# Layer 0's second MLP pair: the right sums' quarters spread over six points, two of them in the pair ahead

## The chip, the cores and the metric

One NeuronCore of a Trainium2 chip runs the whole program. The metric is the device time of one execution in microseconds, taken as the median of several runs; less is better. A profile of one execution is read beside it, and its times count from the first instruction of that execution.

## The reference, cut to what matters

Two layers of each block are run in turn on a tensor x of 2048 x 512: a Fourier mixing block (A) and a token-shift block with an MLP (B).

```
A(x):  a, b = x @ dft_hid_re.T, x @ dft_hid_im.T          # 512 x 512
       y    = dft_seq_re @ a - dft_seq_im @ b              # 2048 x 2048
B(x):  h  = gelu(LN(x) @ w1);  hs = shift(h) @ w2;  x1 = x + hs
       h2 = gelu(LN(x1) @ w3) @ w4;                        # 512 x 1376, 1376 x 512
       return x1 + h2
x = x + A(LN(x));  x = x + B(LN(x));  x = x + A(LN(x));  x = x + B(LN(x))
```

The change touches the end of B in layer 0, where the MLP runs, and there a side job that prepares matrices for A of layer 1.

## The kernel before, in words

**Number format.** Every matrix product is made of three TensorE matmuls (`mm3`, L343 to L345): an operand is split into a high part (a rounding copy on ScalarE, "highs", a CAST in the trace) and a low part (the difference, a subtraction on VectorE, "lows").

**The MLP in pairs.** The 2048 tokens are four chunks of 512, worked in two pairs. In a pair the hidden products of w3 are formed by a seven-product scheme: a period (one turn of `for p in range(NF // 2)`, five in a pair) makes the products b1, b6, b5, b2, b7, then one or two parts of the product with w4 (`w4_part`, T1 and T2 below; the first period has one), then b4 and b3. Each product is six matmuls in the trace into one of four PSUM banks, which are used in turn. A bank comes free when its reader has run: b1 is copied by ScalarE (`u`, L1329), the others are added by VectorE (L567, tile `rest`): `v = u + b6`, `x = v + b5`, `u = u + b2`, `v = v + b7`, `y = v + b5`, later `v = v + b4`, `x = x + b3`. Since four banks go round, b7 waits for the copy of b1, b4 for `v = u + b6`, b3 for `y = v + b5`; the next period's b1, b6, b5 and b2 wait for the additions of b2, b7, b4 and b3.

**The points.** Each engine runs its instructions in the order in which the code is written. Side work is put into that order at points: `one()` takes the next entry of the list `bg`. The second pair has 26 points, 0 to 25: 0 and 1 ahead of the first period, then in each period A (behind the issue of b5), B (behind b7 and its two additions), C and D (behind T1 and T2; the first period has no D) and E (behind b3). So A to E are 2, 3, 4, -, 5 in period 0; 6 to 10 in period 1; 11 to 15, 16 to 20, 21 to 25 in periods 2, 3 and 4. The entries of `bg` there are `lows("t4")` and the list `early`, which normalizes the first rows of the next layer (`xp_stats`, L357 to L363; `xp_norm`, L391; `ax_sums`, L422; `ax_lows`, L448; `ay_sums`, L427).

**The right sums.** `hs_forms` and `hs_quarter` make, in four quarters, seven matrices (`hsd`, in DRAM) out of the four blocks of the hidden DFT matrix; layer 1 reads them from 800 us on. A quarter loads two tiles `m` (blocks b11, b12) and `r` (b21, b22) of 256 KB each (L1210, L1213), forms four sums (L567, output `hp..f` or `hs`), and puts out seven results: high (L1226), low (L1231), and a store of 256 KB to `hsd` (L1232). The results pass through three small buffers `fp[0]`, `fp[1]`, `fp[2]` which lie at the same three places for all quarters; a buffer may be written again only when its store has landed. All transfers are issued by SP, in order, among them the loads of w4 (`w4_load`, L945, 512 KB) and of w3 (`w3_load`, L960, 1792 KB, one at the end of each of the first three periods, ahead of the work of point E).

**Before, a quarter takes five points**, quarter n at points 5n to 5n + 4: the four sums at the first; three highs, the point's own entry and three lows at the second; two results at the third, one each at the fourth and fifth. The loads of the next quarter stand at the end of the fourth (`m`) and fifth (`r`) point. Quarter 0's loads stand in the first pair, in `then[9]`. The list `then` holds work for the first pair's last parts: `then[k + 2]` runs behind part k.

Of the kernel before, what the change touches and what calls it, by code (L numbers as in the profile page):

```python
# [11 lines left out]
ALU = mybir.AluOpType  # L12
# [7 lines left out]
CH = 512  # L20
# [3 lines left out]
DH = D // 2  # L24
# [21 lines left out]
def spectral_mlp_kernel(ctx: ExitStack, tc: tile.TileContext, x, ws, hs, w1, w2, w34, out):  # L46
# [18 lines left out]
    hsd = [[dram.tile([P, 2, CH], F32, name=f"hsd{i}{j}") for j in range(2)] for i in range(7)]  # L65
# [17 lines left out]
    RAWS = EXT + 6 * D  # L83
    STG = RAWS + RAW * 2 * CH + 32
# [3 lines left out]
    def at(name, word, *shape, dtype=F32R):  # L88
        return nc.alloc_sbuf_tensor_at(name, [P, *shape], dtype, offset=base + 4 * word).ap()

    def both(name, word, *shape):
        return at(name, word, *shape), at(name + "f", word, *shape, dtype=F32)
# [134 lines left out]
    raws, slots, sums, place = {}, {}, {}, {}  # L227
# [9 lines left out]
    def rows(sb, d, j, n, load):  # L237
        v = d[j * P : (j + n) * P, :].rearrange("(t p) d -> p t d", p=P)
        nc.sync.dma_start(*((sb, v) if load else (v, sb)))
# [287 lines left out]
    def low(tf):  # L527
        nc.vector.tensor_tensor(tf[0][:, :, 1], tf[1][:, :, 1], tf[0][:, :, 0].bitcast(F32), op=ALU.subtract)
# [37 lines left out]
    def add(o, a, b, op=ALU.add):  # L566
        nc.vector.tensor_tensor(o, a, b, op=op)  # L567
# [292 lines left out]
    def by_pairs(layer, zs, xin, dst):  # L860
# [51 lines left out]
        def sum_of(*names):  # L912
            return lambda: b_sum(*names)
# [4 lines left out]
        def highs(*names):  # L918
            return lambda: [high((blk[b], blkf[b])) for b in names]

        def lows(*names):
            return lambda: [low((blk[b], blkf[b])) for b in names]
# [32 lines left out]
        def w3_load(n):  # L955
            if n >= n_pairs * (NF // 2):
                return
            if layer or n >= NF // 2:
                i = (n + (last_of(layer) and n >= NF // 2)) % 2
                nc.sync.dma_start(w3b[i].bitcast(F32), w3d[n % (NF // 2)])  # L960
                return
            nc.sync.dma_start(staged.rearrange("p f k w -> p f (k w)"), w34[2 * n : 2 * n + 2, :, 0].rearrange("f p w -> p f w"))
# [116 lines left out]
        steps = [(shifted, 0, g) for g in GORDER]  # L1079
# [32 lines left out]
        bg, prep = [], {}  # L1112
# [9 lines left out]
        def do_all(*fs_):  # L1122
            return lambda: [f() for f in fs_]
# [22 lines left out]
        def next_steps():  # L1146

            steps = (
                ((ay_lows, 2), (ay_sums, 3), (ay_highs, 3), (more, 1)),
                ((ay_lows, 3),),  # L1150
                ((xp_stats, 4), (keep_rows, 8)),
                ((xp_stats, 5), (more, 2)),
                ((xp_norm, 4),),
                ((xp_sums, 4), (xp_highs, 4), (more, 3)),
                ((ax_lows, 4), (xp_norm, 5)),
                ((ay_lows, 4), (ax_sums, 5), (ax_highs, 5), (more, 4)),
                ((ax_lows, 5), (keep_rows, 10)),
                ((ahead, 1), (more, len(pieces))),
                ((ahead, 1),),
                ((ahead, 1),),  # L1160
                (),
            )
            return [[do(*s)] for s in steps]
# [30 lines left out]
            ]  # L1194

        def hs_forms():
            steps = []
            for n in range(4):
                d, v = n // 2, slice(n % 2, n % 2 + 1)
                m, r = (at(f"hs{i}{n}", RAWS + (1 + i) * CH, 1, CH, dtype=F32) for i in range(2))  # L1200
                fp = [both(f"hp{i}{n}", word, 1, 2, DH) for i, word in enumerate((RAWS + 3 * CH, STG, STG + CH))]
                steps += hs_quarter(m, r, fp, [(t[d][:, v], hs[(1, d)][:, v], hs[(0, d)][:, v]) for t in hsd])
            return steps

        def hs_quarter(m, r, fp, places):
            b11, b12, b21, b22 = (t[:, :, v] for t in (m, r) for v in (left, right))
            raw = [tf[:, :, 1] for _, tf in fp]

            def load_m():
                nc.sync.dma_start(m, places[0][1])  # L1210

            def load_r():
                nc.sync.dma_start(r, places[0][2])  # L1213

            def sums():
                add(raw[1], b12, b11, ALU.subtract)
                add(raw[2], b22, b12, ALU.subtract)
                add(raw[0], b22, raw[1], ALU.subtract)
                add(b12, raw[0], b21, ALU.subtract)

            def outs(*which):
                which = [(i, n, raw[i] if src is None else src) for i, n, src in which]

                def highs_():
                    for i, _, src in which:
                        act(fp[i][0][:, :, 0], src)  # L1226

                def lows_():
                    for i, n, src in which:
                        t = fp[i][0]  # L1230
                        nc.vector.tensor_tensor(t[:, :, 1], src, t[:, :, 0].bitcast(F32), op=ALU.subtract)  # L1231
                        nc.sync.dma_start(places[n][0].rearrange("p i (l w) -> p i l w", l=2), t.bitcast(F32))  # L1232

                return highs_, lows_

            nothing = lambda: None
            parts = [
                (nothing, sums),
                outs((1, 3, None), (2, 4, None), (0, 2, None)),
                outs((1, 0, b11), (2, 1, b12)),  # L1240
                outs((0, 6, b21)),
                outs((1, 5, b22)),
            ]
            return [(load_m, load_r), *parts]

        def next_block(c, half, to):
            return lambda: b_in(c, half, to)
# [12 lines left out]
        for pair in range(n_pairs):  # L1260
# [10 lines left out]
            if next_too:  # L1271
                hcs[8:] = [hx[:, 0], hx[:, 1], rest[0]]
                bg += [lows("t4"), *early]
                for n in range(4):
                    parts = work[6 * n + 1 : 6 * n + 6]
                    for i, (before, behind) in enumerate(parts):
                        more_ = []
                        if n < 3 and i > 2:
                            more_.append(work[6 * n + 6][i - 3])
                        bg[5 * n + i] = do_all(before, bg[5 * n + i], behind, *more_)  # L1280
            elif pair:
                bg.append(lows("t4"))
            sets = [rest[4:8], rest[4:8]]
# [6 lines left out]
            for i, names in enumerate((("11", "21"), ("12", "22"))):  # L1290
                for d in range(KD):
                    b = blk[names[d // 2]]
                    v = slice(d * P, (d + 1) * P)
# [12 lines left out]
            def next_blocks(*which):  # L1306

                for c, half, to in which:
                    b_in(c, half, to)
# [13 lines left out]
            for p in range(NF // 2):  # L1323
                prep = {} if kept else w_prep(p)
                u, v, x, y = sets[p % 2]
# [49 lines left out]
            then = [[] for _ in range(NF + 2)]  # L1375
            if pair == 0:
                work = hs_forms()
                then[9] = [*work[0]]
                next_blocks((3, 1, "22"))
                then[1] = [lambda: w3_load(NF // 2)]  # L1380
                then[2] = [lambda: rows(xs[0], dst, 0, 2, False)]
                then[3] = [lambda: rows(xs[1], dst, 2, 2, False)]
                then[4] = [sum_of("t1", "12", "11"), sum_of("t2", "22", "t1")]
                then[5] = [sum_of("t3", "22", "12"), sum_of("t4", "21", "t2"), highs("11", "21")]
                names = "11", "21", "12", "22", "t2", "t1", "t3", "t4"
                for i in range(6):
                    then[6 + i] += [lows(names[i]), highs(names[i + 2])]
                then[8] += [lambda: w3_load(NF // 2 + 1)]
                then[12] = [lows("t3")]
            if next_too:  # L1390
                then = next_steps()
            if next_too:
# [497 lines left out]
    for layer in range(LAYERS):  # L1890
# [4 lines left out]
        for c in range(NC):  # L1895
            if layer == 0 and c == 0:
# [22 lines left out]
                def second_low(i):  # L1919
# [5 lines left out]
                parts = [  # L1925
                    [(halves[0][:, 1], mid[0][:, 0], 1), (halves[0][:, 0], ay[0][:, 2], 0)],
                    [(halves[1][:, 0], mid[0][:, 1], 0), (halves[1][:, 1], ay[0][:, 3], 1)],
                ]
# [156 lines left out]
        for i, (ri, dp) in enumerate(HORDER):  # L2085
# [17 lines left out]
            if i == 2:  # L2103
                run_late("re0")
                low(z_half(0, 1))
        by_pairs(layer, zs, xin, out if last_layer else x2d)


# [53 lines left out]
```

## Time and profile before

| what | us |
|---|---|
| median of 3 runs (1448.34 to 1449.6) | 1449.16 |
| the profiled execution, device time | 1448.9 |
| its span, first to last instruction | 1446.9 |
| TensorE matmul busy | 1422.4 (98%) |
| VectorE busy | 1203.9 (83%) |
| ScalarE busy | 731.8 (51%) |

The difference between device time and span, 2.0 us, lies around the program. The second MLP pair of layer 0 runs its periods from 614.7 to 687 us of the span.

In the rows of the profile PE is TensorE, DVE VectorE, ACT ScalarE, POOL GpSimd, and SPq the queue of transfers that SP issues. A row of the timeline gives start, duration, engine, line, operation, output<-inputs, shapes and, in brackets, the idle time before it with what ended it. `hp12f` is the first buffer-written sum of quarter 2, `rest` the tiles u, v, x, y, `psa` and `psd` the four PSUM banks of the products.

### The profile page before, as it was taken

To read this page: it belongs to the slowest core of one execution; us is meant where nothing else is said; L and a number is where in the kernel's file an instruction comes from. 1 tells how busy PE (TensorE), PEld (TensorE's weight loads), DVE (VectorE), ACT (ScalarE), POOL (GpSimd) and SP (SyncE) were. 2 spreads that over 40 slices of the span, in tenths; PEclk is the share of its full clock that TensorE was granted. 3 is DMA by queue.
4 is the path that set the end of the run, shared out by engine and by line. 5 is a ranking of instruction groups with operands and counts; after the bars stand their busy time and mean duration, and the time that the engine had idled before them with its cause. 6 is when DMAs were issued, how large, how long until landed. Compare 5 with 4: busy or idle time off the path is not lost.

```text
span 1446.9 us, 18506 instructions
## 1 busy us (share of the span) xinstructions
PE 1422.4 (98%) x6681; PEld 1190.4 (82%) x6681; DVE 1203.9 (83%) x1725; ACT 731.8 (51%) x1020; POOL 76.7 (5%) x105
## 2 busy tenths in 40 slices
PE   9999999999999999998999999999989999999998
PEld 7888888888888888876888888888877888899887
DVE  7986998989978887677889879879879797897676
ACT  6663454455566654354555434444345656444342
POOL 2100000000002000000000001000000021000000
PEclk9999999999999999999999999999999999999999
DMA  7867657568645858867656667577686447576864
GB/s 253 271 206 237 199 172 262 173 198 297 228 133 155 280 202 286 340 222 282 232 166 211 203 233 248 189 258 250 219 288 234 161 116 262 172 249 219 318 202 165
DMA packets 145628, 325.24 MB, mean 225 GB/s; under 512 B 10624, under 2 KB 61568, under 8 KB 142848
## 3 DMA queue, kind: packets, MB, share of 16 engines
q1 hardware_dynamic: 145536, 324.05, 66.9%
q8 instruction: 53, 0.87, 0.2%
q14 instruction: 39, 0.32, 0.1%
HBM read 262.41 MB, written 61.60 MB: 224 GB/s over the span
## 4 chain that ended last, share of the span: by engine, by line
PE 79%; DVE 10%; DMA 4%; ACT 3%; issue 2%; SPq 0%; POOL 0%; DVEq 0%; ACTq 0%; POOLq 0%
PE psd L343 8%; PE psd L345 8%; PE psd L344 8%; PE psa L344 7%; PE psa L343 7%; PE psa L345 6%; PE psb L344 6%; PE psb L345 6%; PE psb L343 6%; PE psc L344 6%; PE psc L345 6%; PE psc L343 6%; DVE ring L300 2%; DMA raw<-in_ws 1%; DVE rest L567 1%
## 5 line engine op out<-in xcount | busy, mean ns | idle before, releaser
L300 DVE TENSOR_TENSOR ring<-raw,ring 128x1024 fp32r<-128x1024 f32 x102 | 124.2, 1220 | 19.1 <-ACT ring L279 19.0
L279 ACT CAST ring<-raw 128x1024 fp32r<-128x1024 f32 x103 | 107.9, 1051 | 55.0 <-PE psd L345 24.9
L383 POOL TENSOR_TENSOR rs<-ve,mhalf 128x4 f32<-128x4 f32 x16 | 26.9, 1684 | 741.0 <-DVE nm L382 741.0
L300 DVE TENSOR_TENSOR ring<-ring1f,ring 128x512 fp32r<-128x512 f32 (+1 forms) x56 | 53.3, 952 | 2.9 <-ACT ring L282 2.9
L286 ACT CAST ring<-ring2f 128x1024 fp32r<-128x1024 f32 x28 | 29.6, 1056 | 49.9 <-DVE ring2f L285 49.9
L343 PE MATMUL psd<-rawr,hf 128*128 128x256 f32 x168 | 49.1, 292 | 5.8 <-issue 4.8
L286 ACT CAST ring<-ring0f 128x1024 fp32r<-128x1024 f32 x28 | 29.5, 1053 | 47.0 <-DVE ring0f L285 46.6
L391 ACT ACTIVATE tmp<-xs,nb,rs 128x512 f32<-128x512 f32 x56 | 43.3, 809 | 19.0 <-POOL nb L363 13.5
L343 PE MATMUL psc<-ring,ay 128*128 128x512 f32 x128 | 50.0, 391 | 2.2 <-ACT rr11f L610 2.2
L362 POOL TENSOR_TENSOR rs<-ve,mhalf 128x2 f32<-128x2 f32 (+2 forms) x33 | 29.6, 898 | 425.4 <-DVE nb L361 406.5
L344 PE MATMUL psb<-ring,ay 128*128 128x512 f32 x128 | 49.9, 390 | 2.2 <-DVE ring L300 2.2
L300 DVE TENSOR_TENSOR ring<-ring3f,ring 128x1024 fp32r<-128x1024 f32 (+1 forms) x50 | 49.3, 986 | 3.1 <-ACT ring L282 2.6
L344 PE MATMUL psc<-ring,ay 128*128 128x512 f32 x128 | 49.9, 390 | 0.6 <-DVE ring L300 0.6
L343 PE MATMUL psd<-ring,ay 128*128 128x512 f32 x126 | 49.4, 392 | 0.6 <-DVE tmp L567 0.6
L345 PE MATMUL psc<-ring,ay 128*128 128x512 f32 x128 | 49.8, 389 | 0.0
L343 PE MATMUL psb<-ring,ay 128*128 128x512 f32 x128 | 49.8, 389 | 0.0
L345 PE MATMUL psb<-ring,ay 128*128 128x512 f32 x128 | 49.8, 389 | 0.0
L344 PE MATMUL psd<-ring,ay 128*128 128x512 f32 x126 | 49.0, 389 | 0.0
L344 PE MATMUL psa<-ring,ay 128*128 128x512 f32 x126 | 49.0, 389 | 0.0
L345 PE MATMUL psd<-ring,ay 128*128 128x512 f32 x126 | 49.0, 389 | 0.0
L343 PE MATMUL psa<-ring,ay 128*128 128x512 f32 x126 | 49.0, 389 | 0.0
L345 PE MATMUL psa<-ring,ay 128*128 128x512 f32 x126 | 49.0, 389 | 0.0
(896 smaller groups left out, 4763.6 us busy)
## 6 DMA issues: line engine op xcount, KB each, us to landing
raw<-in_ws SPq DMA_DIRECT2D x183, 512.0 KB, 5.3
w4r<-w4d SPq DMA_DIRECT2D x44, 512.0 KB, 5.2
rawr<-hsd SPq DMA_DIRECT2D x42, 512.0 KB, 4.8
w3b<-w3d SPq DMA_DIRECT2D x10, 1792.0 KB, 9.5
raw<-in_hs SPq DMA_DIRECT2D x32, 512.0 KB, 3.9
w3d<-w3b SPq DMA_DIRECT2D x5, 1792.0 KB, 7.0
hsd<-hp SPq DMA_DIRECT2D x28, 256.0 KB, 2.5
x1d<-tmp SPq DMA_DIRECT2D x12, 512.0 KB, 7.4
```

What stands on the lines that cost most here:

```text
L279: nc.scalar.copy(dest[:, a:b, 0], r[0][:, a:b])
L286: nc.scalar.copy(dest[:, :, 0], lo)
L300: nc.vector.tensor_tensor(lo, src, hi.bitcast(F32), op=ALU.subtract)
L343: nc.tensor.matmul(o, lh, rh, start=first, stop=False, skip_group_check=more)
L344: nc.tensor.matmul(o, lh, rl, start=False, stop=False, skip_group_check=more)
L345: nc.tensor.matmul(o, ll, rh, start=False, stop=last, skip_group_check=more)
L362: nc.gpsimd.tensor_tensor(rs[:, :n], ve[:, :n], mhalf[:, 0, :n], op=ALU.pow)
L383: nc.gpsimd.tensor_tensor(rs, ve, mhalf[:, :, :2], op=ALU.pow)
L391: nc.scalar.activation(o, s, AF.Identity, bias=mr[2], scale=mr[1])
L567: nc.vector.tensor_tensor(o, a, b, op=op)
```

## The change

A quarter is cut into six parts. The first sum (b12 - b11, into `fp[0]`) stands alone; the next part puts that result out, with the other three sums between its high and its low; the remaining parts put out two, one, two and one results. Quarter n begins at point 6n - 2, so that quarter 0 has its first two parts in the first pair (`then[11]` and `then[12]`), and the others start at points 4, 10 and 16. The three buffers change roles from quarter to quarter (`words[(i + n) % 3]`). The next quarter's `m` is loaded ahead of the point before its first part, and `r` behind that point's work. The numbers of instructions are unchanged on every engine.

```
         def hs_forms():
-            steps = []
+            work = []
...
-                fp = [both(f"hp{i}{n}", word, 1, 2, DH) for i, word in enumerate((RAWS + 3 * CH, STG, STG + CH))]
-                steps += hs_quarter(m, r, fp, [(t[d][:, v], hs[(1, d)][:, v], hs[(0, d)][:, v]) for t in hsd])
-            return steps
+                words = (RAWS + 3 * CH, STG, STG + CH)
+                fp = [both(f"hp{i}{n}", words[(i + n) % 3], 1, 2, DH) for i in range(3)]
+                work.append(hs_quarter(m, r, fp, [(t[d][:, v], hs[(1, d)][:, v], hs[(0, d)][:, v]) for t in hsd]))
+            return work
...
+            def first_sum():
+                add(raw[0], b12, b11, ALU.subtract)
+
             def sums():
-                add(raw[1], b12, b11, ALU.subtract)
-                add(raw[2], b22, b12, ALU.subtract)
-                add(raw[0], b22, raw[1], ALU.subtract)
-                add(b12, raw[0], b21, ALU.subtract)
+                add(raw[1], b22, b12, ALU.subtract)
+                add(raw[2], b22, raw[0], ALU.subtract)
+                add(b12, raw[2], b21, ALU.subtract)
...
             parts = [
-                (nothing, sums),
-                outs((1, 3, None), (2, 4, None), (0, 2, None)),
-                outs((1, 0, b11), (2, 1, b12)),
-                outs((0, 6, b21)),
-                outs((1, 5, b22)),
+                ((), (first_sum,)),
+                ((high_,), (sums, low_)),
+                part((1, 4, None), (2, 2, None)),
+                part((0, 0, b11)),
+                part((1, 1, b12), (2, 6, b21)),
+                part((0, 5, b22)),
             ]
...
-                for n in range(4):
-                    parts = work[6 * n + 1 : 6 * n + 6]
+                ahead_, behind_ = [[] for _ in bg], [[] for _ in bg]
+                for n, (load_m, load_r, parts) in enumerate(work):
+                    at_ = 6 * n - 2
+                    if n:
+                        ahead_[at_ - 1].append(load_m)
+                        behind_[at_ - 1].append(load_r)
                     for i, (before, behind) in enumerate(parts):
-                        more_ = []
-                        if n < 3 and i > 2:
-                            more_.append(work[6 * n + 6][i - 3])
-                        bg[5 * n + i] = do_all(before, bg[5 * n + i], behind, *more_)
+                        if at_ + i >= 0:
+                            ahead_[at_ + i] += before
+                            behind_[at_ + i] += behind
+                bg[:] = [do_all(*f, g, *h) for f, g, h in zip(ahead_, bg, behind_)]
...
-                then[9] = [*work[0]]
+                then[9] = [*work[0][:2]]
...
-                then[12] = [lows("t3")]
+                then[11] += work[0][2][0][1]
+                then[12] = [*work[0][2][1][0], lows("t3"), *work[0][2][1][1]]
```

How the order of instructions moves at three places. First VectorE at the end of the first pair, ahead of the additions of its last result into the rows (`xs`, L1110); `hs_4384` is quarter 0's m, `hs_4385` its r, and `bt_..` are operands of the second pair.

```order
 L528 TENSOR_TENSOR bt_228<-bt1f,bt_228 128x2x512
+L567 TENSOR_TENSOR hp00f<-hs_4384 128x256
 L528 TENSOR_TENSOR bt_232<-bt3f,bt_232 128x2x512
+L567 TENSOR_TENSOR hp10f<-hs_4385,hs_4384 128x256
+L567 TENSOR_TENSOR hp20f<-hs_4385,hp00f 128x256
+L567 TENSOR_TENSOR hs_4384<-hp20f,hs_4385 128x256
+L1234 TENSOR_TENSOR hp_4386<-hp00f,hp_4386 128x256
 L1110 TENSOR_TENSOR xs_165<-psc_285,xs_165 128x512
```

Four sums and one low now stand ahead of the additions into the rows; before, none of them did.

Second VectorE in period 3 (points A, B and C of the last quarter's start); `xs_166` is the row tile that `xp_stats` reads, `rest_..` the additions x, u, v, y, and `hp03f`, `hp13f`, `hp23f`, `hs_4408` the sums of quarter 3. The first rows are the end of its statistics.

```order
 L361 TENSOR_SCALAR nb<-mv 128x2
-L1231 TENSOR_TENSOR hp_4412<-hp13f,hp_4412 128x256
-L1231 TENSOR_TENSOR hp_4414<-hp23f,hp_4414 128x256
-L1231 TENSOR_TENSOR hp_4410<-hp03f,hp_4410 128x256
+L567 TENSOR_TENSOR hp03f<-hs_4408 128x256
 L567 TENSOR_TENSOR rest_278<-rest_277,psd_287 128x512
 L567 TENSOR_TENSOR rest_276<-rest_276,psa_280 128x512
 L567 TENSOR_TENSOR rest_277<-rest_277,psa_281 128x512
 L567 TENSOR_TENSOR rest_279<-rest_277,psd_287 128x512
```

Three lows leave this place; the first sum of quarter 3, which reads that quarter's m, now stands ahead of the four additions x, u, v and y.

Third SP at the end of period 2, around the last load of w3 (`w3b_238<-w3d_87`); `hs_4408` and `hs_4409` are m and r of quarter 3.

```order
 L945 DMA w4r_249<-w4d_117 128x1024
-L1232 DMA hsd_100<-hp_4404 128x512
-L1213 DMA hs_4409<-in_hs 128x512
+L1235 DMA hsd_92<-hp_4404 128x512
+L1235 DMA hsd_102<-hp_4406 128x512
 L960 DMA w3b_238<-w3d_87 128x3584
-L1232 DMA hsd_96<-hp_4412 128x512
-L1232 DMA hsd_98<-hp_4414 128x512
-L1232 DMA hsd_94<-hp_4410 128x512
+L1211 DMA hs_4408<-in_hs 128x512
+L1235 DMA hsd_100<-hp_4402 128x512
+L1214 DMA hs_4409<-in_hs 128x512
```

Before, both loads of quarter 3 were issued ahead of the load of w3; now both stand behind it. Those of quarters 1 and 2 stand ahead of their period's load of w3 in both kernels.

More of the change, by code (lines that the diff above doesn't have):

```diff
@@ L1234, in outs, with part @@
                 return highs_, lows_
-            nothing = lambda: None
+            def part(*which):
+                high_, low_ = outs(*which)
+                return (high_,), (low_,)
+            high_, low_ = outs((0, 3, None))
             parts = [
-                (nothing, sums),
-                outs((1, 3, None), (2, 4, None), (0, 2, None)),
-                outs((1, 0, b11), (2, 1, b12)),
-                outs((0, 6, b21)),
-                outs((1, 5, b22)),
+                ((), (first_sum,)),
[4 more added lines that the diff above has]
+                part((0, 5, b22)),
             ]
-            return [(load_m, load_r), *parts]
+            return load_m, load_r, parts
         def next_block(c, half, to):
```

## The prediction

> **What bounds the kernel now.** I read first the page's shares, then the stretch of the second pair in windows, then who waited for whom there. TensorE is busy 98% of the span, so only its idle time and its slow time can be won.
>
> ```profile
> PE   1422.4 (98%) x6681; PEld 1190.4 (82%) x6681; DVE 1203.9 (83%) x1725; ACT 731.8 (51%) x1020; POOL 76.7 (5%) x105
> ```
>
> (The page's own first line; the next two are windows, with busy time and instruction count of each engine, then clock.)
>
> ```profile
> 600.00:638.00 38.00, 38.00 (x169) 31.48 (x168) 25.82 (x51) 14.01 (x26) 1.09 (x3) 1.00 0.66 243
> 615.00:690.00 75.00, 69.18 (x288) 55.42 (x287) 55.36 (x122) 36.90 (x73) 4.02 (x8) 0.95 0.71 249
> ```
>
> The first window has no stall: 169 matmuls in 38.00 us, 0.225 us each. The second holds the five periods: its 288 matmuls would need 64.8 of the 75 us, so about 10 us are lost. Where, the timeline of TensorE shows (start, duration, the idle time in brackets):
>
> ```profile
> 641.41 0.50 PE L343 MATMUL psa<-b,w3b 128*128 128x512 f32 x1 [0.74 <-DVE rest L567]
> 646.43 0.50 PE L343 MATMUL psa<-bt,w3b 128*128 128x512 f32 x1 [0.64 <-DVE rest L567]
> 660.68 0.80 PE L343 MATMUL psa<-b,w3b 128*128 128x512 f32 x1 [3.07 <-DVE rest L567]
> 661.27 0.63 PE L344 MATMUL psa<-b,w3b 128*128 128x512 f32 x1
> ...
> 666.39 0.56 PE L344 MATMUL psd<-bt,w3b 128*128 128x512 f32 x1
> 666.79 0.39 PE L345 MATMUL psd<-bt,w3b 128*128 128x512 f32 x1
> 679.47 0.50 PE L343 MATMUL psd<-b,w3b 128*128 128x512 f32 x1 [0.73 <-DVE rest L567]
> 684.50 0.50 PE L343 MATMUL psd<-bt,w3b 128*128 128x512 f32 x1 [0.64 <-DVE rest L567]
> ```
>
> Five times PE waits for an addition `rest` that frees a bank. The first, third and fourth are b3 waiting for `y`, the others the next b5 waiting for `v + b4`. The idle time sums to 5.8 us; the third stall is dearer than it looks, because behind 3.07 us of idleness the 14 matmuls from 660.68 to 666.79 stand 6.1 us apart instead of 3.2. With about 0.3 us more at the refilling behind each short stall (0.50 us for its first matmul), the loss is 5.8 + 2.9 + 1.3 = 10.0 us, as the count says.
>
> Why are the additions late? The waits of this stretch (engine, line, waited for: total, times, longest):
>
> ```profile
> DVE hp12f L567 <- DMA hsd<-hp: 3.7, 1, 3.7
> DVE hp13f L567 <- DMA hsd<-hp: 3.2, 1, 3.2
> DVE hp11f L567 <- DMA hsd<-hp: 2.4, 1, 2.4
> ACT hp L1226 <- DMA hsd<-hp: 4.9, 5, 3.2
> DVE hp23f L567 <- DMA hs<-in_hs: 0.2, 1, 0.2
> ```
>
> Once a quarter VectorE stands at the first sum until the store that last used its buffer has landed, and everything behind it in order, the additions too, is late by as much. For quarter 2:
>
> ```profile
> 652.99 0.43 DVE L567 TENSOR_TENSOR hp12f<-hs 128x256 f32<-128x256 f32 x1 [3.71 <-DMA hsd<-hp]
> 653.53 0.43 DVE L567 TENSOR_TENSOR hp22f<-hs,hs 128x256 f32<-128x256 f32 x1
> 655.27 1.28 DVE L357 BATCH_NORM_STATS2 st<-xs 128x6 f32<-128x512 f32 x2
> 657.02 0.42 DVE L1231 TENSOR_TENSOR hp<-hp12f,hp 128x256 fp32r<-128x256 f32 x1
> 659.94 0.69 DVE L567 TENSOR_TENSOR rest<-rest,psa 128x512 f32<-128x512 f32 x1
> ```
>
> The reader is to see the queue: sums, statistics, three lows, and only at 659.94 the addition y, which ends at 660.6; b3 starts at 660.68.
>
> **The change part by part.** *Removed.* A buffer was written again one point after its last store's issue; with the rotated roles two points lie between. All three waits of a first sum for a store go, and so would all five stalls: at most **-10.0 us**.
>
> *What is late next.* With nothing stalled, PE would run b1 of period 1 at 626.91 and a period in 66 matmuls, 15.0 us (b3 of period 1 at 640.5, of period 2 at 655.5, of period 3 at 670.4). I walk VectorE's order along that clock with the trace's own durations:
>
> ```profile
> 657.69 0.42 DVE L1231 TENSOR_TENSOR hp<-hp02f,hp 128x256 fp32r<-128x256 f32 x1
> 658.02 1.28 DVE L567 TENSOR_TENSOR rest<-rest,psa 128x512 f32<-128x512 f32 x2
> 659.22 0.68 DVE L567 TENSOR_TENSOR rest<-rest,psd 128x512 f32<-128x512 f32 x1
> ...
> hsd<-hp SPq DMA_DIRECT2D x1, 256.0 KB, 2.0
> ```
>
> From start to start an addition holds VectorE for 0.60 us (658.02 to 659.22 for two), one that needs the addition before it 0.72 (659.22 to 659.94), a sum or low of 256 columns 0.34 (657.02 to 657.69 for two), the statistics 1.75 (655.27 to 657.02); a store with nothing ahead lands in 2.0. Quarter 1's r is issued at about 625 and lands at about 630; sums, v, statistics, two lows, x, u, v, y end at 637.0, 3.5 us ahead of b3. In period 2 m lands at 647.3 and y ends at 653.8, 1.7 us ahead of b3. So the dearest stall is gone. Behind it, point D now holds two lows whose highs wait for the stores of point B (655.6 plus 2.0); `v + b4` ends at 659.7, b5 of period 3 is due at 659.55, and the ScalarE copy of b1 stands behind a gelu: I take **+0.4 us**.
>
> *Period 3* has the term that matters. Quarter 3's m now stands behind the load of w3 on SP. What that does, the trace shows where it stands so already (SP's issues, and then, in the same order, the KB of each and its us to landing):
>
> ```profile
> 579.87 0.43 SPq L960 DMA_DIRECT2D w3b<-w3d  x1
> 582.22 0.32 SPq L945 DMA_DIRECT2D w4r<-w4d  x1
> 582.64 0.38 SPq L239 DMA_DIRECT2D x2d<-xs  x1
> 598.91 0.59 SPq L1210 DMA_DIRECT2D hs<-in_hs  x1
> 627.43 0.43 SPq L1210 DMA_DIRECT2D hs<-in_hs  x1
> ...
> w3b<-w3d SPq DMA_DIRECT2D x1, 1792.0 KB, 10.7
> w4r<-w4d SPq DMA_DIRECT2D x1, 512.0 KB, 9.6
> x2d<-xs SPq DMA_DIRECT2D x1, 512.0 KB, 10.5
> hs<-in_hs SPq DMA_DIRECT2D x1, 256.0 KB, 6.9
> hs<-in_hs SPq DMA_DIRECT2D x1, 256.0 KB, 3.5
> ```
>
> The w4 load landed 1.2 us after the w3 load issued 2.4 us ahead of it: transfers land nearly in order. In the walk the stores of point D of period 2 leave at 659.1, the w3 load at 659.5, m at 659.9. I bound m's landing by 3.5 us (quarter 1's m, nothing large ahead) and 10.5 us (x2d, two places behind a w3 load), 663.4 to 670.4, and take 9.3, nearest to the 9.6 of the transfer behind a w3 load: 669.2. VectorE stands there from 665.2, the end of the statistics. Then first sum, x, u, v, y: 0.34 + 3 x 0.60 + 0.72 = 2.9, so y at 672.1; b3 is due at 670.4 + 0.4: **+1.3**. Behind it come r's three sums, high, normalization (ScalarE, 1.52, in its row below), ax sums, two lows, one low, and `v + b4` ends at 677.2; b5 of period 4 is due at 674.5 + 1.7 = 676.2: **+1.0**. At point E two highs wait for stores and stand ahead of ScalarE's copy of b1, for which b7 waits: **+0.5**.
>
> ```profile
> 680.59 1.52 ACT L391 ACTIVATE xs<-xs,nb,rs 128x512 f32<-128x512 f32 x2
> ```
>
> *The tail.* Quarter 3 now reaches into period 4, one low more ahead of a dense VectorE stretch; VectorE is ahead by 6.3 us there against PE's 6.8. The stall below may grow by the difference: **+0.5**.
>
> ```profile
> 708.54 0.50 PE L345 MATMUL psd<-w4r,h 128*128 128x512 f32 x1 [0.18 <-DVE h L768]
> ```
>
> *The first pair.* Four sums and a low, 0.42 + 3 x 0.34 + 0.34 = 1.8 us, go ahead of the additions into the rows; the first must wait for m (issued 598.91, 6.9 to landing: 605.8), and `lows("t3")` with it.
>
> ```profile
> 607.39 0.69 DVE L1110 TENSOR_TENSOR xs<-psc,xs 128x512 f32<-128x512 f32 x1 [3.12 <-PE psc L345]
> 613.43 0.69 DVE L768 TENSOR_TENSOR h<-tmp,h 128x512 fp32r<-128x512 f32 x1 [3.31 <-ACT h L771]
> 621.47 0.39 PE L343 MATMUL psc<-w4r,h 128*128 128x512 f32 x1
> ```
>
> The additions would start at 608.7 instead of 607.39 and end at 611.1. VectorE's next work waits for ScalarE until 613.43, and the banks they free are used again at 621.47: **0**. That cover goes only if m lands 2.3 us later. SP's two stores of rows there wait behind the first quarter store, 1.3 us, with nothing due.
>
> *Sum:* -10.0 + 0.4 + 1.3 + 1.0 + 0.5 + 0.5 = -6.3 us against the profiled execution's 1448.9 (span 1446.9 and 2.0 around it): 1442.6. That execution lies 0.26 us under the median of the runs shown, so I say **1442.7 us**. The bounds of m's landing: at 663.4 only the 0.4 and perhaps 0.5 remain, 1439.4 to 1439.8; at 670.4 the stall of b3 grows by 1.2, 1443.9.
>
> **A rule weighed.** The Trainium skill, page "DMA: Bandwidth & Descriptors", section "Anatomy of one DMA", fits a transfer as 2.0 us plus bytes over 436 GB/s, there for the GpSimd path. By that estimate the w3 load would land after 6.2 us and m 0.6 us later, at 666.3 instead of 669.2, and the two largest terms would go: 1440.3. The rows here give 10.7 and 9.6 us with little ahead of them, so I keep 9.3. This is the first rival's price from another side.
>
> **The rivals.** *(1) All stalls go.* m of quarter 3 lands by 667, as m and r of quarters 0 to 2 did (3.5 to 6.9 us), and y is in time. For it: VectorE's slack of 1.7 us and more in periods 1 and 2. Against it: the order on SP. Time 1448.9 - 10.0 + 0.4 = 1439.3.
>
> *(2) The loads take the stores' place.* The stores were not much later than r: in the rows above the second sum of quarter 2 starts 0.54 us behind the first, when r had landed, and quarter 3 waits 0.2 for it. If m or r of quarter 2 lands 3 us later than I walk, y of period 2 is late by 1.3 and `v + b4` behind it by 3: about 3 us more lost, 1445.7. Against it: loads leave earlier, since SP no longer stands behind late lows.
>
> *(3) The slow clock comes back, and the kernel gets slower.* VectorE standing at the first sum of quarter 3 idles PE at b3. If m lands 1.9 us later than my 669.2, that idleness reaches the 3.07 us at which the trace shows the granted clock at 0.5, and 2.9 us are added: 1448.9 - 6.3 + 1.9 + 2.9 = 1447.4. The kernel is slower than before from 1.5 us later still, m landing 12.7 us after its issue, and by 2.9 us from 15.6. The row of 10.5 us speaks against that. The Trainium skill, page "TensorE: Matmul & The Clock Gate", Part 1, puts the fall of the clock behind about 3.4 us of idleness; in this trace 3.07 sufficed, so this rival begins 0.3 us sooner than by the page.
>
> *(4) Nothing is gained:* the order shows sums and stores moved, but if VectorE is late for its own work (55.4 of 75 us) more than for the waits, the same lateness stays, 1448.9.
>
> **How the numbers follow.** Forecast 0.50, (1) 0.20, (2) 0.15, (3) 0.07, (4) 0.08. A measurement of this kernel tells about 0.2% from no change, 2.9 us. Forecast, (1) and most of (2) are faster: 0.82; (4) and the rest of (2) the same: 0.11; (3) slower: 0.07. The range takes in (1), with 0.8 us below for the small stalls at 646 and 708, and (2): 1438.5 to 1446.5; (3) and (4), 0.15, are left out.
>
> **What the profile would show.** Right: no wait of a sum for hsd<-hp; no PE idleness over 0.5 us before period 3; the clock 1.00 throughout; a wait of `hp03f` for hs<-in_hs of about 4 us and PE idle 1 to 1.5 us behind it; the additions into the rows about 1.3 us later in the first pair, without PE idle. Wrong: if `hp03f` waits for nothing, rival (1); if `hp02f` or the sums of quarter 1 wait for loads over 2 us, rival (2).

## The result, and the profile after

| | before | after |
|---|---|---|
| median, us | 1449.6 (1448.34 to 1450.34, 9 runs) | 1445.77 (1444.61 to 1446.35, 9 runs) |
| profiled execution, device time / span, us | 1448.9 / 1446.9 | 1444.61 / 1442.6 |

The ratio of the medians is 0.9978, with a 95% interval of 0.9969 to 0.9986: 2.0 to 4.5 us faster, where 6.5 was forecast. The direction was right, the gain about half.

The two windows that were shown of before, now of after (busy time and count of PE, PEld, DVE, ACT, POOL, then clock, DMA share, GB/s):

```profile
615.00:690.00 75.00, 70.11 (x306) 56.76 (x305) 56.33 (x121) 38.90 (x74) 4.08 (x8) 1.00 0.73 251
600.00:638.00 38.00, 38.00 (x169) 31.49 (x168) 29.32 (x59) 16.92 (x31) 2.16 (x4) 1.00 0.75 268
```

In the same 75 us TensorE now does 306 matmuls instead of 288, at full clock; at 0.227 us each, their spacing where nothing stalls, they need 69.5, so some 5.5 us are still lost there. Four rows of TensorE's timeline behind 655 us say where (start, duration, idle time before in brackets):

```profile
660.89 0.50 PE L343 MATMUL psd<-bt,w3b 128*128 128x512 f32 x1 [1.18 <-DVE rest L567]
673.88 0.50 PE L343 MATMUL psd<-b,w3b 128*128 128x512 f32 x1 [1.81 <-DVE rest L567]
680.13 0.50 PE L343 MATMUL psd<-bt,w3b 128*128 128x512 f32 x1 [1.87 <-DVE rest L567]
705.98 0.50 PE L345 MATMUL psd<-w4r,h 128*128 128x512 f32 x1 [1.26 <-DVE h L768]
```

The stalls at 641, 646 and 660 us, with the slow clock behind the last, are gone. In their place come b5 of period 3, b3 of period 3, b5 of period 4 and the tail. The waits of VectorE and ScalarE between 600 and 720 us (total, times, longest):

```profile
ACT hp L1229 <- DMA hsd<-hp: 6.3, 6, 2.0
DVE hp03f L567 <- DMA hs<-in_hs: 4.4, 1, 4.4
DVE hp00f L567 <- DMA hs<-in_hs: 3.3, 1, 3.3
DVE hp02f L567 <- DMA hs<-in_hs: 2.9, 1, 2.9
```

No sum waits for a store (`hsd<-hp`) any more; three first sums wait for their load, and six highs on ScalarE wait for stores.

Laid one over the other, matmul by matmul, the two timelines give the shift of after against before. It was taken at each matmul where it changes; the rows at the stalls are quoted here or in the prediction.

| matmul, start after | shift, us | change | forecast |
|---|---|---|---|
| until 640 | 0.0 | | |
| behind the three stalls removed, 658.65 | -8.1 | -8.1 | -8.0 |
| b5 of period 3, 660.89 | -6.8 | +1.3 | +0.4 |
| b3 of period 3, 673.88 | -5.6 | +1.2 (2.1 lost, 0.9 before) | 1.3 lost |
| b5 of period 4, 680.13 | -4.4 | +1.2 (2.1 lost, 0.9 before) | 1.0 lost |
| b7 of period 4, 683.18 | -4.2 | +0.2 | +0.5 |
| tail, 696.26 and 705.98 | -2.6 | +1.6 | +0.5 |
| same place in layer 1, 800 | -2.6 | | -6.3 |

Here -2.6 us stand where -6.3 were forecast; the profiled executions differ by 4.3 in all, the medians by 3.8. The other 1.7 arise in layer 1, whose instructions are the same. One place of it, behind the same idle stretch of 2.00 us (before, then after):

```profile
860.92 0.36 PE L343 MATMUL psd<-rawr,hf 128*128 128x256 f32 x1 [2.00 <-issue]
...
861.59 0.42 PE L344 MATMUL psd<-rawr,hf 128*128 128x256 f32 x1
```

```profile
858.33 0.36 PE L343 MATMUL psd<-rawr,hf 128*128 128x256 f32 x1 [2.00 <-issue]
...
858.88 0.28 PE L344 MATMUL psd<-rawr,hf 128*128 128x256 f32 x1
```

The second rows are the same matmul: 0.42 us at half clock in before's execution, 0.28 in after's. Elsewhere in layer 1 it was the other way round. Such places differ from one execution to the next, so below I compare kernels by two numbers: the ratio of times, and the **local shift**, that of the same matmul against before's profile at 740 us (-2.6 for after), behind the changed stretch and ahead of layer 1.

### The profile page after: what moved, and what is told of

Same layout as the page of the kernel before. It is cut to its first block, busy times and chain, and to the rows that moved or that the text cites. A ratio compares the mean times of both kernels' runs of the same rounds, so it can differ in the third digit from the quotient of the medians.

```text
span 1442.6 us, 18504 instructions
## 1 busy us (share of the span) xinstructions
PE 1419.6 (98%) x6681; PEld 1189.0 (82%) x6681; DVE 1203.5 (83%) x1725; ACT 731.6 (51%) x1020; POOL 76.3 (5%) x105
## 4 chain that ended last, share of the span: by engine, by line
PE 78%; DVE 11%; DMA 4%; ACT 3%; issue 2%; SPq 0%; POOL 0%; DVEq 0%; ACTq 0%; POOLq 0%
PE psd L343 8%; PE psd L345 8%; PE psd L344 8%; PE psa L345 6%; PE psa L344 6%; PE psa L343 6%; PE psb L344 6%; PE psb L345 6%; PE psb L343 6%; PE psc L344 6%; PE psc L345 6%; PE psc L343 6%; DVE ring L300 2%; DMA raw<-in_ws 2%; DMA hs<-in_hs 1%
```

## The experiments

Which of the terms that the walk set too low did so, and why? Two theories, and a rival. **L**: the load of quarter 3's `m`, and of `r`, stands behind the load of w3 on SP; VectorE stands at the first sum until it lands, and the additions behind it free banks late. **S**: the stores land later than the walk's 2.0 us; highs on ScalarE wait for them, then lows on VectorE, then the additions. The rival is that VectorE's own work is the limit, so that no transfer matters.

**Quarter 3's `m` ahead of the w3 load** (`m_early`: all `m` are loaded one point sooner, behind the point before):

```
-                        ahead_[at_ - 1].append(load_m)
+                        behind_[at_ - 2].append(load_m)
```

> The changed kernel, with each quarter's m loaded one point sooner, behind the point whose low last reads it, so that quarter 3's m stands ahead of the load of w3 on SP. Theory L (the wait for quarter 3's m behind the w3 load, 4.4 us, is what was mis-sized): m lands by 666.5, the stall of b3 in period 3 (1.8 us idle) goes, r still lands behind w3 at about 672 so the stall of b5 in period 4 stays over 1 us; 2.6 us less than the changed kernel, about 1443.2. Theory S (the waits of the highs for stores make VectorE late): 1 us less at most, 1444.8. Theory B (VectorE has simply too much work in a period): no difference, 1445.5 to 1446.

Measured: 1442.08 us, ratio 0.9959 [0.9945, 0.9972], local shift -5.5. The first sum and, of the same timeline of VectorE, the second:

```profile
665.34 0.42 DVE L567 TENSOR_TENSOR hp03f<-hs 128x256 f32<-128x256 f32 x1
671.35 0.43 DVE L567 TENSOR_TENSOR hp13f<-hs,hs 128x256 f32<-128x256 f32 x1 [3.07 <-DMA hs<-in_hs]
```

`m`, issued 0.55 us ahead of the w3 load, landed 5.6 us after its issue and the first sum waits for nothing; b3 of period 3 stalls no more. The wait has moved to `r`, which is still behind the w3 load, and with it one stall stays (b5 of period 4, 1.89 us). L is borne out, the rival falls. The stall of b5 in period 3, of which the expectation does not speak, is gone too: quarter 2's `m` was also issued sooner, `hp02f` starts at 646.81 instead of 647.84, and `v + b4` behind it at 659.15 instead of 660.16, though highs wait for stores here no less than in the change (7.3 us in all).

**A place of its own for each result** (`own_places`), in quarters 1 to 3; loads as in the change:

```
-                words = (RAWS + 3 * CH, STG, STG + CH)
-                fp = [both(f"hp{i}{n}", words[(i + n) % 3], 1, 2, DH) for i in range(3)]
+                X, Y, Z = RAWS + 3 * CH, STG, STG + CH
+                words = (
+                    (X, Y, Z, X, Y, Z, X),
+                    (Y, Z, X, XS, XS + CH, XS - 2 * CH, XS - CH),
+                    (Z, X, Y, Z, XS + CH, XS + 2 * CH, XS + 3 * CH),
+                    (W12 + 6 * CH, Y, Z, X, RNG + 8 * CH, RNG + 9 * CH, RNG + 10 * CH),
+                )[n]
+                fp = [both(f"hp{i}{n}", words[i], 1, 2, DH) for i in range(7)]
...
-                part((0, 0, b11)),
-                part((1, 1, b12), (2, 6, b21)),
-                part((0, 5, b22)),
+                part((3, 0, b11)),
+                part((4, 1, b12), (5, 6, b21)),
+                part((6, 5, b22)),
```

> The changed kernel with places of their own for the results of quarters 1 to 3, so that no high waits for a store; loads as in the changed kernel. Theory S: the stall of b5 in period 3 (1.2 us idle) goes, the additions of period 3 come 2.5 us sooner behind y, the stall of b5 in period 4 (1.9 us) goes, b3 in period 3 still stalls 2 us for m: 4 us less, about 1441.5. Theory L: only the stall of b5 in period 3 goes, 1.4 us less, 1444.4. Theory B: no difference.

Measured: 1443.98 us, ratio 0.9972 [0.9961, 0.9982], local shift -4.4. ScalarE's waits for stores fell from 6.3 us to one of 0.2. TensorE's stalls in periods 3 and 4, and VectorE's row at the first sum of quarter 3:

```profile
673.61 0.50 PE L343 MATMUL psd<-b,w3b 128*128 128x512 f32 x1 [2.93 <-DVE rest L567]
679.11 0.50 PE L343 MATMUL psd<-bt,w3b 128*128 128x512 f32 x1 [1.08 <-DVE rest L567]
```

```profile
670.62 0.43 DVE L567 TENSOR_TENSOR hp03f<-hs 128x256 f32<-128x256 f32 x1 [5.66 <-DMA hs<-in_hs]
```

The stall of b5 in period 3 is gone and that of b5 in period 4 is down from 1.87 to 1.08 us. In period 3 `v + b4` starts 1.5 us sooner (658.67); 0.6 of that is `hp02f`, which also starts sooner (647.24), so the stores make about 0.9 of it. But `m` lands when it lands (670.6 instead of 670.9), so VectorE and TensorE, both earlier, wait the longer for it: b3 stalls 2.93 us instead of 1.81. With hardly a wait for a store left, 1.8 us are gained, and the time is nearer to L's 1444.4 than to S's 1441.5; the largest stall that is left waits for a load.

**The roles alone** (before, with the change's rotation and its five points) and **the six points alone** (the change, with before's fixed places):

```
-                fp = [both(f"hp{i}{n}", word, 1, 2, DH) for i, word in enumerate((RAWS + 3 * CH, STG, STG + CH))]
+                words = (RAWS + 3 * CH, STG, STG + CH)
+                fp = [both(f"hp{i}{n}", words[(i + n) % 3], 1, 2, DH) for i in range(3)]
```

> The kernel before with one part of the change, the three buffers changing roles from quarter to quarter; five points a quarter, all in the second pair, as before. If the waits for stores are what cost, the first two sums no longer wait, but the third writes where the last store of the quarter ahead went out one point earlier, and the second needs r, which landed 0.5 us behind that store: 1447.5 to 1449. If the roles bring the gain of the change: 1446.

```
-                fp = [both(f"hp{i}{n}", words[(i + n) % 3], 1, 2, DH) for i in range(3)]
+                fp = [both(f"hp{i}{n}", words[i], 1, 2, DH) for i in range(3)]
```

> The changed kernel without the change of roles: six points, two of them in the pair ahead, but the three buffers at fixed places. The first sum of a quarter then writes where b22's store left one point earlier: by the landings of the changed kernel (625.2 + 3.2, 642.5 + 5.9, 664.1 + 7.4) it waits until 628.4, 648.4 and 671.5, that is 0.6 us longer than for m in quarters 2 and 3. If the spreading brings the gain: 1446 to 1447.5. If the roles bring it: 1449 or more.

Measured: 1448.33 us, ratio 0.9999 [0.9989, 1.0009], and 1448.28 us, ratio 0.9998 [0.9990, 1.0007]; local shifts +0.6 and +1.1. Neither half brings anything. VectorE's waits of the roles alone, then of the six points alone:

```profile
DVE hp23f L567 <- DMA hs<-in_hs: 2.8, 1, 2.8
DVE hp22f L567 <- DMA hs<-in_hs: 2.3, 1, 2.3
DVE hp12f L567 <- DMA hs<-in_hs: 1.5, 1, 1.5
```

```profile
DVE hp03f L567 <- DMA hsd<-hp: 5.6, 1, 5.6
DVE hp02f L567 <- DMA hsd<-hp: 3.2, 1, 3.2
DVE hp01f L567 <- DMA hsd<-hp: 1.9, 1, 1.9
```

With the roles alone no sum waits for a store, but with four sums at one point they wait for `r` (and `m`) instead, at the same place and about as long. With the six points alone the places come round too soon, and the sums wait for the stores. The change needs both: it is the separation of the first sum from the others, with places whose store is two points old, that pays.

**The loads of quarters 2 and 3 well ahead** (`loads_early`: quarter 2's tiles get other places, so that quarter 3's are free early; the loads are issued behind points 8 and 10, the last of them a whole period ahead of the third w3 load):

```
-                m, r = (at(f"hs{i}{n}", RAWS + (1 + i) * CH, 1, CH, dtype=F32) for i in range(2))
+                m, r = (at(f"hs{i}{n}", (XS + 2 * CH if n == 2 else RAWS + CH) + i * CH, 1, CH, dtype=F32) for i in range(2))
...
-                    if n:
+                    if n == 1:
                         ahead_[at_ - 1].append(load_m)
                         behind_[at_ - 1].append(load_r)
+                    elif n:
+                        behind_[8 if n == 2 else 10] += [load_m, load_r]
```

> The changed kernel with both loads of quarter 2 into other places behind point 8 and both loads of quarter 3 behind point 10, so that neither waits behind the w3 load of period 2; results in the shared places, as in the changed kernel. Theory L: no sum of quarters 2 and 3 waits for a load, y of period 3 ends near 669.3 and v + b4 near 674.3, both in time; all stalls of periods 2 to 4 go: about 1440. Theory S: the highs still wait 0.8 to 1.8 us for stores, the two stalls of b5 stay at 1 us or more: 1442 to 1443.

Measured: **1439.68 us**, ratio 0.9942 [0.9928, 0.9957], local shift -8.2. The window of the periods, and all stalls that are left behind 655 us:

```profile
615.00:690.00 75.00, 74.56 (x329) 61.40 (x329) 61.05 (x129) 41.65 (x79) 4.19 (x8) 1.00 0.76 260
```

```profile
660.08 0.50 PE L343 MATMUL psd<-bt,w3b 128*128 128x512 f32 x1 [0.44 <-DVE rest L567]
700.30 0.50 PE L345 MATMUL psd<-w4r,h 128*128 128x512 f32 x1 [1.24 <-DVE h L768]
```

329 matmuls in 75 us, 41 more than before: the periods are nearly without a stall, though highs still wait 6.5 us for stores here. Such waits cost little when the loads leave VectorE ahead. Quarter 3's two loads stand behind a w3 load here too, that of period 1, and land 10 us after their issue; but that is by 655, and the first sum starts at 665.5. This version is faster than before and than the change (whose ratio was 0.9978, with an interval from 0.9969), as L expected and S did not.

**Both remedies together**, first with `m` one point sooner, then with all loads well ahead; each is the sum of the diffs above (in the second, quarter 2's places are `(Z, X, Y, Z, XS + CH, W12 + 7 * CH, Z)`, since its loads take two of the others).

> m one point sooner and places of their own together. r of quarter 3 still lands behind w3 at about 671, so the three sums of quarter 3 wait some 3 us, as they did with m one point sooner (1442.1); without the waits for stores v + b4 of period 3 comes 1 us sooner, the stall of b5 in period 4 falls from 1.9 to about 0.9 us: 1441. If the two effects simply add (-3.7 and -1.8 us to the changed kernel): 1440.3.

> Loads early and places of their own: nothing of the side work waits for a transfer. Theory B (VectorE has too much work in periods 2 to 4): a stall of b3 or b5 stays there, over 0.5 us. Theories L and S: none of them stays, the 10 us of the kernel before are gone up to the stall near 705 for the low of h, which comes from VectorE's own work in period 4: 1438.5 to 1440.

Measured: 1440.31 us, ratio 0.9939 [0.9926, 0.9953], local shift -7.8; and 1444.43 us, ratio 0.9963 [0.9949, 0.9977], local shift -4.6. The first adds as expected, to 0.5 us in the local shift (-2.6 - 2.9 - 1.8 = -7.3). The second missed its expectation, for a reason of its own; ScalarE's row and then TensorE's:

```profile
664.90 0.63 ACT L765 ACTIVATE hc<-rest 128x512 f32<-128x512 f32 x1 [4.71 <-DMA hsd<-hp]
```

```profile
666.36 0.50 PE L343 MATMUL psa<-bt,w3b 128*128 128x512 f32 x1 [3.89 <-ACT rest L1349]
```

The place that I borrowed belongs to a tile into which a gelu writes in period 3. That gelu waited for the store, the copy of b1 stood behind it, and TensorE idled 3.89 us. It says nothing on L and S, but it is the cleanest case here of a store that costs: not because it is slow, but because the next writer of the place has a bank to free right behind.

**Before once more**, for the spread of its own stalls (no edit).

> The kernel before, unchanged, profiled once more. If the half clock behind the 3.07 us of idleness at 660.7 belongs to that idleness, it is there again and the periods lose 10 us again. If it depends on when the idleness falls, the same stall may stand without it, and the periods lose about 7 us.

Measured: 1448.69 us. The dearest stall, with the clock halved again:

```profile
661.64 0.80 PE L343 MATMUL psa<-b,w3b 128*128 128x512 f32 x1 [3.57 <-DVE rest L567]
```

3.57 us where the first profile had 3.07; the local shift is +1.0. So the removal is worth 10 to 11 us, and a local shift is good to about 1 us.

**The tail.** A wait of 0.96 to 1.26 us for `h` is in the change and in every faster version above but `loads_early` with places of their own, where TensorE comes late for the stall of 3.89 us. It is in the six points alone too (1.25 us), where TensorE comes to it when it does in before (708.3 and 708.4). `loads_early` with quarter 3's last two parts left out (points 20 and 21; three of the 28 results are not computed, their stores stay):

```
+            if last:
+                parts[4:] = [stale((1, 1), (2, 6)), stale((0, 5))]
```

> loads_early with the last two parts of quarter 3 (three highs on ScalarE and three lows on VectorE, at the last point of period 3 and the first of period 4) left out; their stores stay, out of what the buffers held, so three of the 28 results are not computed. Theory P: the stall of about 1.2 us ahead of the last w4 product (matmul waiting for the h sum of line 768), which is in every version that is faster than before, comes from these three lows and highs, about 1.0 us of VectorE that the change pushed into period 4. Then the stall falls to 0.3 us or less, and the time to about 1438.5 (1 us less than loads_early, 1439.7). Rival U: it comes from VectorE's and ScalarE's own chain of period 4 (sums that wait for ScalarE, then the additions that free banks, then h), which is late against a TensorE that comes earlier. Then the stall stays at 0.9 us or more and the time at 1439.3 to 1440.

Measured: 1440.92 us, ratio 0.9939 [0.9927, 0.9951], local shift -8.1. The tail's wait was 0.18 us, but TensorE also came 1.2 us later, for an earlier stall (b5 of period 4, 1.34 us). Both theories can claim that, and against `loads_early` (ratio 0.9942) the medians show none of the 1 us that P expected. So both kernels ran once more, side by side.

> The kernel of last_parts_out once more (last two parts of quarter 3 left out, their stores kept). In its profile b5 of period 4 stalled for 1.34 us because a store landed late, ahead of the part that was left out, so that TensorE came to the tail 1.06 us later than in loads_early and the short wait there (0.18) said nothing. Theory P: if that stall is absent this time, the wait for h ahead of the last w4 product is still 0.3 us or less, and the matmul behind it starts near 699.3 us. Rival U: the wait is 0.9 us or more, and it starts near 700.3 us.

> The kernel of loads_early once more, beside last_parts_out_again. Theory P and rival U alike: wait for h about 1.2 us, the matmul behind it near 700.3 us if b5 of period 4 does not stall; if it stalls by more than 1 us, as in last_parts_out, P says a wait of 1.2 us at about 701.5, U a wait below 0.3 us at 700.4.

Measured: 1438.21 and 1439.8 us (one execution each), local shifts -9.3 and -7.2. First TensorE of the kernel with the parts left out, then of `loads_early` again:

```profile
675.15 0.50 PE L343 MATMUL psd<-bt,w3b 128*128 128x512 f32 x1 [0.48 <-DVE rest L567]
...
698.67 0.39 PE L344 MATMUL psd<-w4r,h 128*128 128x512 f32 x1
699.19 0.50 PE L345 MATMUL psd<-w4r,h 128*128 128x512 f32 x1
```

```profile
675.82 0.50 PE L343 MATMUL psd<-bt,w3b 128*128 128x512 f32 x1 [0.80 <-DVE rest L567]
...
701.36 0.50 PE L345 MATMUL psd<-w4r,h 128*128 128x512 f32 x1 [1.24 <-DVE h L768]
```

Without the parts the matmul starts 0.52 us behind its predecessor, at 699.19; with them it waits 1.24 us, and does so although TensorE is itself later than in the first `loads_early`. P is borne out, on one execution of each. From one sum `h` to the pair that the matmul waits for, VectorE needs the same time either way (rows of the same execution of the kernel with the parts out, then of the first execution of `loads_early`):

```profile
688.73 0.69 DVE L768 TENSOR_TENSOR h<-tmp,h 128x512 fp32r<-128x512 f32 x1 [0.28 <-ACT h L778]
...
698.46 1.28 DVE L768 TENSOR_TENSOR h<-hc,h 128x512 fp32r<-128x512 f32 x2
```

```profile
689.85 0.69 DVE L768 TENSOR_TENSOR h<-tmp,h 128x512 fp32r<-128x512 f32 x1 [0.75 <-ACT h L778]
...
699.57 1.28 DVE L768 TENSOR_TENSOR h<-hc,h 128x512 fp32r<-128x512 f32 x2
```

9.73 and 9.72 us, as in before and after: nothing of that chain was caught up. `loads_early` enters it 1.1 us later, with the three lows and the waits with them, and leaves it 1.1 us later.

## Why the prediction was half right

*The removal, -10.0:* right. By 658.65 the shift is -8.1, the two stalls of 0.9 us behind it are replaced by others, and the version with the least stall, that with the last parts left out, reaches -9.3 with 0.48 us of idleness remaining.

*The first pair, 0:* right. The additions started at 609.34, not 608.7, for `m` landed 0.6 us later; TensorE has no idle time there.

```profile
606.40 0.43 DVE L567 TENSOR_TENSOR hp00f<-hs 128x256 f32<-128x256 f32 x1 [3.27 <-DMA hs<-in_hs]
...
609.34 0.69 DVE L1110 TENSOR_TENSOR xs<-psc,xs 128x512 f32<-128x512 f32 x1
```

*Periods 1 and 2:* right for b3, which runs at 655.47 without a stall. But y of period 2 starts at 653.91, where I had its end at 653.8: `m` of quarter 2 came 0.5 us later than walked (`hp02f` at 647.84 for 647.3), and y ended 0.8 us late. The slack took that at b3; it did not take it further on.

**The step that failed** is the walk behind it, from point D of period 2 on: "two lows whose highs wait for the stores of point B (655.6 plus 2.0); `v + b4` ends at 659.7". The mechanism is the one named, with `hp03f` waiting 4.4 us for its load where "about 4 us" was said, but its sizes are not: PE then idled 1.81 us, where "1 to 1.5" was said. The rows of ScalarE, VectorE and SP there:

```profile
658.14 0.41 ACT L1229 CAST hp<-hs 128x256 fp32r<-128x256 f32 x1 [0.55 <-DMA hsd<-hp]
659.38 0.41 ACT L1229 CAST hp<-hs 128x256 fp32r<-128x256 f32 x1 [0.83 <-DMA hsd<-hp]
```

```profile
659.82 0.42 DVE L1234 TENSOR_TENSOR hp<-hs,hp 128x256 fp32r<-128x256 f32 x1 [0.80 <-ACT hp L1229]
660.16 0.68 DVE L567 TENSOR_TENSOR rest<-rest,psd 128x512 f32<-128x512 f32 x1
...
670.89 0.42 DVE L567 TENSOR_TENSOR hp03f<-hs 128x256 f32<-128x256 f32 x1 [4.44 <-DMA hs<-in_hs]
```

```profile
660.68 0.43 SPq L960 DMA_DIRECT2D w3b<-w3d  x1
661.16 1.28 SPq L1211 DMA_DIRECT2D hs<-in_hs  x1
```

```profile
w3b<-w3d SPq DMA_DIRECT2D x1, 1792.0 KB, 9.5
hs<-in_hs SPq DMA_DIRECT2D x1, 256.0 KB, 9.7
```

Both highs wait for the stores of point B: 2.0 us after its issue I had from one store with nothing ahead, for a store that leaves at 655.6. The two left late, as y was, from 656.04 on; the first landed after 2.0 us, the second after 2.9, and they were waited for until 658.14 and 659.38. The second low waits for its high, and `v + b4` ends at 660.8 instead of 659.7. **That is the +1.3 at b5 in place of +0.4.** Load and stores share in it: the stall went in `m_early`, where `hp02f` starts 1.0 us sooner, and in `own_places`, where the highs hardly wait for stores and `hp02f` starts 0.6 us sooner. The low's store is issued by SP ahead of the w3 load, so SP, too, is late: the w3 load at 660.68 for 659.5, `m` at 661.16 for 659.9. `m` lands 9.7 us after, where I had 9.3, so at 670.9 for 669.2. **That is the 2.1 at b3 in place of 1.3.** My bounds of the landing, 663.4 to 670.4, held the duration but counted from a fixed issue time. In front of `v + b4` of period 4, VectorE waits once more for a high that waits for a store (1.79 us), which I had left out: 680.1 instead of 677.2, of which 1.7 were there already in y. **That is 2.1 in place of 1.0** at b5: with the store waits gone, in `own_places`, the stall there is 0.8 us shorter.

*The tail, +0.5:* a counting error. I wrote "one low more"; the last two parts are three highs and three lows, at points 20 and 21, and quarter 3 ended at 19 before. Left out they give 1.1 us back; with the rest of the lateness it was 1.6.

The five terms were put at +3.7 and measured +7.3. The time lies within the range, and beside *rival (2)* at 1445.7, which is luck: it had `m` or `r` of quarter 2 land 3 us late, and `hp02f` started 0.5 us later than walked. The sign that I had set for it, a wait of `hp02f` for its load of over 2 us, did show (2.93), but it was set too low: even with `m` at the walk's 647.3 the wait would have been 2.4. *Rival (1)*, all stalls gone at 1439.3, is where `loads_early` (1439.68) ends: what I put against it, the order on SP, is what had to be changed. *Rival (3)*: the clock stayed at 1.00 in the periods, as forecast. *Rival (4)* falls with `m_early`.

The estimate by the rule that I had weighed, of the Trainium skill, "DMA: Bandwidth & Descriptors", "Anatomy of one DMA", put `m` at 666.3; it landed at 670.9. What fits is another section of that page: the Trainium skill, "DMA: Bandwidth & Descriptors", "Queues, rings and completion order", says that each DMA engine consumes the descriptors of a queue in ring order. A 256 KB load issued 0.5 us behind the 1792 KB of w3 landed after 9.7 us, and 0.55 us ahead of it after 5.6. No run here shows the rings themselves.

How far the stores' lateness varies, with the same code, remains open: ahead of the part left out, `loads_early` and the kernel of `last_parts_out` are alike, and in four executions the third sum of quarter 3 waited for a store not at all, 1.7, 2.2 and 2.5 us, with 0 to 1.34 us of stall at b5 of period 4 behind it. Rows of the executions with 2.5 and with none (there it waits for a high):

```profile
DVE hp23f L567 <- DMA hsd<-hp: 2.5, 1, 2.5
```

```profile
DVE hp23f L567 <- ACT hp L1229: 0.7, 1, 0.7
```

That store is issued behind the w3 load, which may be the reason; no run moved it ahead.

## What to carry to other kernels

When a walk along an in-order engine puts small latenesses at nothing, let each one run on: a late low delayed a store's issue, the store's issue the next load on the same queue, and that load the additions, so a load that landed 0.5 us late in one period became a load 1.7 us late and, with one more wait for a store, an addition 2.9 us late in the next. Look first at what stands behind the largest transfer of a queue, and load early what the critical engine will meet in order; that was worth 5.7 us of local shift beyond the change's own 2.6. Parts that are moved later in a list must be counted to the last one, for they come out in a stretch that had no slack.

## What the runs showed of the hardware

The clock does not fall at a fixed length of idleness. In one execution (the roles alone) TensorE stalled twice for nearly the same time:

```profile
660.69 0.50 PE L343 MATMUL psa<-b,w3b 128*128 128x512 f32 x1 [2.99 <-DVE rest L567]
661.03 0.39 PE L344 MATMUL psa<-b,w3b 128*128 128x512 f32 x1
...
679.82 0.80 PE L343 MATMUL psd<-b,w3b 128*128 128x512 f32 x1 [2.93 <-DVE rest L567]
680.41 0.63 PE L344 MATMUL psd<-b,w3b 128*128 128x512 f32 x1
```

Behind 2.99 us the matmuls kept their 0.39 us; behind 2.93 they took 0.63, as they do behind before's 3.07. In `own_places` 2.93 us left the clock whole, and the 2.00 us in layer 1 above halved it in one execution and not in the other. My rival (3) used 3.07 us as a threshold, which it is not. Nor need the clock fall where the matmuls begin again. Behind the 3.89 us of `loads_early` with places of their own the first three matmuls ran at full clock, and it halved at the fourth, 0.8 us later:

```profile
666.69 0.39 PE L344 MATMUL psa<-bt,w3b 128*128 128x512 f32 x1
...
667.53 0.63 PE L344 MATMUL psa<-bt,w3b 128*128 128x512 f32 x1
```

The Trainium skill, "TensorE: Matmul & The Clock Gate", Part 1, tells of a free-running window of activity, of about 3.4 us; a window whose place differs would fit one stall that halves the clock and an equal one that does not, though stalls of 2.93 and 3.07 us are shorter than the idle window that it names. No run here shows the window itself.
